# Two recurrent chains: summing head groups on VectorE after the transposes, instead of on TensorE before them

## The chip, the cores and the metric

The kernel runs on one core of one Trainium2 chip. Times are device microseconds (us) of one launch; the profile is one profiled execution of the same program. TensorE is called PE in the profile, its weight loads PEld, VectorE DVE, ScalarE ACT, GpSimd POOL; SPq is the queue of SyncE, from which most DMA transfers of this kernel are issued, in the order of the program.

## The reference, cut to what matters

The program computes a value and all its gradients. The part that decides here is a recurrence over 64 segments of 32 rows, with 8 memory rows handed from each segment to the next:

```python
for s in range(n_seg):                      # 64 segments, one after another
    h = concat([mem, x[s*32:(s+1)*32]])     # 8 + 32 rows of 512
    q, k, v = h@Wq, h@Wk, h@Wv              # 32 heads of 128
    p = softmax(mask(q@k.T * scale))
    o = einsum('bhte,hed->btd', p@v, Wo)    # a sum over 32 heads
    mem = o[:, :8]                          # the next segment waits for this
    outs.append(o[:, 8:])
```

The gradient runs the same chain backwards: the gradient of the eight memory rows is handed from segment s to segment s-1. There is also a dense squared-ReLU branch, which the change doesn't touch.

## The kernel before

The kernel has six stages: the dense branch, the projections of everything that doesn't depend on the memory ("left"), the forward chain (about 500 to 1375 us), a left backward stage, the backward chain (about 1605 to 2606 us), and the weight gradients. Each chain has 64 steps. Four steps make a block, which shares loads and "left" work (operations with the prefix `L.`). Steps are numbered 0 to 3 within a block, in order of execution.

The sum over 32 heads at the end of a step is made in two parts. TensorE adds up eight heads for each of four head groups, so that the result R lies in one PSUM bank with the groups on different partitions: 4 groups x 32 rows = 128 partitions, 512 columns. The four groups are then added, and the result turned so that the 512 columns lie on partitions, as the next projection wants them:

```python
def sum_ops(o, alloc, R4, F, st, pre=""):
    def sm():                                  # add the four groups: sel is a 0/1 matrix, 128 x 32
        ps["n"] = alloc("ps_sum")
        for c in range(DC):                    # 4 column blocks of 128
            nc.tensor.matmul(ps["n"][SEG*c:SEG*c+SEG, 0:P], lhsT=sel[:],
                             rhs=R4()[:, c*P:(c+1)*P], start=True, stop=True, ...)
    def sF():                                  # PSUM -> SBUF, 128x128
        ps["F"] = F()
        ENGS[pre + "sF"](ps["F"][:], ps["n"][:, 0:P])
    def sT():                                  # one float32 transpose
        nc.tensor.transpose(ps["n"][:, P:2*P], ps["F"][:], identF[:])
        st["sum"] = ps["n"][:, P:2*P].rearrange("p (c r) -> p c r", c=DC)
    ...
def ra():                                      # PSUM -> SBUF, all 512 columns, on ScalarE
    st["R4"] = fo.tile([P, D], F32, name="R4", tag="R4s")
    ENGS["ra"](st["R4"][:], ps["R"][:])
def HTf():                                     # the next memory rows: X (forward) or GT (backward)
    ENGS["HT"](block(b1)["X"][:, :, j1*SEG:j1*SEG+M], st["sum"][:, :, 0:M])
o["xt"] = lambda: ENGS["xt"](B_["XT"][:, :, j, M:SEG], st["sum"][:, :, M:SEG])   # the other 24 rows
```

The order in which operations are issued is written by hand, one string for each of the four steps. Each engine executes its own operations in that order. The strings end with the tail of the step: `ra sm sF sT HT`.

Of the kernel before, what the change touches and what calls it, by code (L numbers as in the profile page):

```python
# [8 lines left out]
ALU = mybir.AluOpType  # L9
AX = mybir.AxisListType  # L10
BF16 = mybir.dt.bfloat16
# [15 lines left out]
def kernel(  # L27
# [126 lines left out]

    sel = const.tile([P, SEG], F32, name="sel")
    nc.vector.tensor_reduce(sel[:], identF[:].rearrange("p (g r) -> p r g", g=HG), axis=AX.X, op=ALU.add)
# [325 lines left out]
    def sum_ops(o, alloc, R4, F, st, pre=""):  # L482

        ps = {}

        def sm():
            ps["n"] = alloc("ps_sum")
            for c in range(DC):
                nc.tensor.matmul(ps["n"][SEG * c:SEG * c + SEG, 0:P], lhsT=sel[:], rhs=R4()[:, c * P:(c + 1) * P],  # L489
                                 start=True, stop=True, tile_position=(0, SEG * c), skip_group_check=True)  # L490

        def sF():
            ps["F"] = F()
            ENGS[pre + "sF"](ps["F"][:], ps["n"][:, 0:P])

        def sT():
            nc.tensor.transpose(ps["n"][:, P:2 * P], ps["F"][:], identF[:])
            st["sum"] = ps["n"][:, P:2 * P].rearrange("p (c r) -> p c r", c=DC)
        o["sm"], o["sF"], o["sT"] = sm, sF, sT
# [92 lines left out]
    def play(order, n, steps, lefts, step, blk, last={}):  # L592
# [20 lines left out]
        "q0mm xt- L.lv L.ex0 q0ev L.mst- k0mm L.mx1 L.sb1 L.ex1 k1mm k1ev q1mm q0fl k0ev L.su0 k0fl L.su1 "  # L613
        "q1ev L.rc0 k1fl q0Te L.lq+ q1fl k0Te soP- k1Te s0 q1Te mx0 L.pm0 s1 km sb0 mx1 ex0 L.sm- soV- sb1 "
        "L.sF- soN ex1 v1mm ld- v0mm su0 rc0 su1 rc1 pm0 L.sT- ld tu0 pm1 tu1 kl+ v1ev L.lm v0ev L.ldL+ w0 "
        "L.xt- ob0 L.BT- oa0 L.rc1 soP L.tu0 w1 ob1 g0 oa1 g1 ra L.W0 sm L.out- L.oa0 sF L.ob0 sT HT",
        "k0mm L.hl++ L.pm1 q1mm q0mm ld k0ev xt- q1ev q0ev k1mm soV- k0fl q0fl L.tu1 k1ev k0Te q1fl q0Te k1fl k1Te s0 "
        "q1Te mx0 sb0 km s1 mx1 L.W1 ex0 sb1 su0 rc0 L.ob1 kl+ soN ex1 v0mm v0ev su1 L.oa1 v1mm pm0 rc1 tu0 w0 "
        "v1ev pm1 tu1 ob0 oa0 soV w1 ob1 g0 oa1 L.t3 g1 ra sm sF sT HT",
        "q0mm k0mm xt- q1mm k1mm q0ev q0fl q1ev k0ev soP- q0Te k0fl q1fl k1ev k1fl k0Te s0 q1Te k1Te mx0 L.u0- "  # L620
        "sb0 s1 v0mm mx1 sb1 ex0 ex1 su0 v0ev rc0 v1mm L.u3 su1 L.G0 rc1 pm0 pm1 L.t2 tu0 v1ev tu1 w0 ob0 L.t1 "
        "oa0 w1 g0 oa1 ob1 L.sx- L.ra0 L.u2 soP ld km g1 ra sm soN sF sT HT",
        "q0mm k0mm L.hs+ q0ev k1mm xt- q1mm q0fl k0ev kl q0Te k0fl k1ev k1fl L.u1 L.otr L.lo q1ev q1fl k0Te s0 k1Te "
        "q1Te mx0 s1 sb0 soV- ex0 L.t0 mx1 km sb1 su0 ex1 v1mm kl+ v0mm rc0 su1 rc1 pm0 tu0 L.mtr L.G1 v1ev "
        "v0ev pm1 tu1 L.lb w0 ob0 soN oa0 L.S0+ L.mx0+ w1 g0 oa1 ob1 g1 L.sb0+ ra L.ra1 sm sF L.S1+ sT HT")
    ENGS = on_engines(
        "L.oa0 L.oa1 L.ob0 L.ob1 L.sF L.xt k1Te k1ev oa1 ob0 q0ev q1ev ra v0ev v1ev",
        "HT L.pm0 L.pm1 L.ra0 k0Te k0ev oa0 ob1 pm0 pm1 q0Te q1Te sF xt")
    with sb("fw", 1) as fw, psum("fr", 4) as fr, psum("fpp", 1) as fpp, \
# [47 lines left out]
        def block(b):  # L677

            if b not in blk:
                shapes = {"kL": (fs, [P, KH, HG, NL], BF16), "OT": (fs, [P, HG, KH, SPB, SEG], BF16),  # L680
                          "X": (fs, [P, DC, P], BF16),
                          "kM": (fo, [P, KH, HG, NL], BF16), "vTM": (fo, [P, KH, HG, NL], BF16),
                          "XT": (fs, [P, DC, SPB, SEG], F32), "qL": (fo, [P, KH, HG, NL], BF16),
                          "VL": (fo, [P, GW], BF16), "vM": (fo, [P, GW], BF16), "EL": (fo, [P, KH, KW], BF16),
                          "OTL": (fo, [P, KH, HG, NL], BF16),
                          "bb": (fo, [P, D], BF16), "R4": (fo, [P, D], F32), "F": (fo, [P, P], F32)}

                def make(n):
                    pool, shape, dt = shapes[n]
                    return pool.tile(shape, dt, name=n, tag=n)  # L690
                blk[b] = Tiles(make)
            return blk[b]

        def left(b):
# [22 lines left out]
            for p in range(2):  # L717
# [21 lines left out]
                def G_(p=p):  # L739
# [5 lines left out]
            sum_ops(o, big, lambda: B_["R4"], lambda: B_["F"], st, "L.")  # L745
            o["xt"] = lambda: ENGS["L.xt"](B_["XT"][:, :, :, 0:M],
                                                st["sum"].rearrange("p c (j t) -> p c j t", j=SPB))
# [32 lines left out]
        def fwd(s):  # L780
# [80 lines left out]
            def ra():  # L861
                st["R4"] = fo.tile([P, D], F32, name="R4", tag="R4s")
                ENGS["ra"](st["R4"][:], ps["R"][:])
            o["ra"] = ra
            sum_ops(o, big, lambda: st["R4"], lambda: fo.tile([P, P], F32, name="F", tag="Fs"), st)

            def HTf():
                if s + 1 < NSEG:
                    b1, j1 = divmod(s + 1, SPB)
                    ENGS["HT"](block(b1)["X"][:, :, j1 * SEG:j1 * SEG + M], st["sum"][:, :, 0:M])  # L870
            o["HT"] = HTf
            o["xt"] = lambda: ENGS["xt"](B_["XT"][:, :, j, M:SEG], st["sum"][:, :, M:SEG])
# [40 lines left out]
    with sb("ls", 3) as ls, sb("lo", 1) as lo_, psum("lpp", 1) as lpp, psum("lr", 4) as lr:  # L913
# [87 lines left out]
        "o0mm o0ev xt- L.xt- o1mm o0fl vp0 L.lq o1ev o0te o1fl s0 vea0 veb0 o1te ldq- ldn- L.qo ldk- vtr vg0 "  # L1001
        "vlb0 d10 vla0 vp1 d20 d30 s1 L.G0 veb1 L.H0 d11 vlb1 vla1 d40 vea1 d21 tu0 kp0 kea0 klb0 keb0 d31 vg1 "
        "d41 kla0 qp0 qea0 qeb0 ldp kg0 tu1 kp1 kea1 klb1 L.sx- keb1 kla1 qg0 qp1 ldn qea1 qeb1 L.ra0 kg1 qg1 "
        "ra L.G1 sm vc sF L.H1 sT HT",
        "L.ra1 o0mm ldk- o1mm o0ev vtr o0fl o0te vp0 veb0 xt- o1ev vlb0 vla0 L.ktr vea0 s0 o1fl vp1 o1te L.G2 "
        "d10 d20 veb1 s1 vlb1 d30 vg0 d40 vea1 tu0 ldq- vla1 kp0 vg1 d11 kea0 kla0 d21 klb0 keb0 d31 d41 L.vtr "
        "qp0 qeb0 ldp qea0 tu1 vc kg0 kp1 kea1 qg0 keb1 kla1 klb1 qp1 kg1 qeb1 qea1 qg1 L.H2 ra sm sF sT L.ra2 "
        "HT",
        "xt- o0mm o0ev o1mm o0fl o1ev ldn- ldq- ldk- vp0 o1fl o0te s0 vlb0 veb0 d10 vla0 vea0 d20 d30 o1te vp1 "
        "vg0 vlb1 vtr s1 L.G3 vc vla1 veb1 d40 vea1 tu0 L.vst d11 d21 kp0 klb0 kea0 keb0 kla0 d31 vg1 L.kst d41 "  # L1010
        "qp0 qeb0 qea0 tu1 kg0 kp1 kea1 keb1 qg0 kla1 klb1 qp1 L.qtr kg1 qeb1 qea1 qg1 ra L.H3 sm sF sT ldp ldn "
        "HT",
        "L.ra3 o0mm L.qst o0ev L.ldt+ o1mm xt- o0fl L.gl+ o1ev vp0 o1fl o0te vlb0 vea0 vla0 s0 veb0 o1te vp1 "
        "d10 d20 d30 veb1 s1 d11 vg0 ldk- vlb1 d40 tu0 vea1 vtr L.gs+ vla1 ldq- d21 L.sm kp0 klb0 vc vg1 keb0 "
        "d31 L.sF kea0 kla0 d41 qp0 L.vo+ qeb0 tu1 kg0 qea0 L.ldv+ kp1 qg0 keb1 kla1 klb1 kea1 qp1 L.ldk+ qeb1 "
        "qea1 ldp kg1 L.ko+ qg1 ra sm sF L.sT sT HT")
    ENGS = on_engines(
        "L.ra0 L.sF kea0 kea1 kla0 kla1 o0ev o1ev o1te qea0 qeb1 ra sF vea0 vea1 veb1 vla0 vla1 vlb1 "
        "xt",
        "HT L.xt keb0 keb1 klb0 klb1 o0te qea1 qeb0 veb0 vlb0")  # L1020
    with sb("bq", 1) as bq, sb("bs", 2) as bs, sb("bt", 1) as bt, psum("bpp", 1) as bpp, psum("br", 4) as br:
# [11 lines left out]
        def block(b):  # L1033
            if b not in blk:
                shapes = {"gkL": (bs, [P, KH, HG, NL], BF16), "gvL": (bs, [P, KH, HG, NL], BF16),
                          "gqL": (bt, [P, KH, HG, NL], BF16), "PG": (bt, [P, 1, KH, KW], BF16), "GL": (bt, [P, 1, KH, KW], BF16),
                          "gOL": (bt, [P, GW], BF16), "qNL": (bt, [P, GW], BF16), "vTL": (bt, [P, KH, HG, NL], BF16),
                          "XT": (bs, [P, DC, SPB, SEG], F32), "R4": (bt, [P, D], F32), "F": (bt, [P, P], F32),
                          "gv": (bt, [P, HG, KH, SPB, SEG], BF16), "gk": (bt, [P, HG, KH, SPB, SEG], BF16),
                          "gq": (bt, [P, HG, KH, SPB, SEG], BF16)}  # L1040

                def make(n):
                    pool, shape, dt = shapes[n]
                    return pool.tile(shape, dt, name="b_" + n, tag=n)
                blk[b] = Tiles(make)
            return blk[b]

        def left(b):
# [15 lines left out]
            for i in range(4):  # L1064
# [12 lines left out]
                else:  # L1077
                    o["ra%d" % i] = lambda i=i: nc.vector.tensor_tensor(out=B_["R4"][:], in0=ps["R", i][:],
                                                                        in1=B_["R4"][:], op=ALU.add)
            sum_ops(o, big, lambda: B_["R4"], lambda: B_["F"], st, "L.")  # L1080
            o["xt"] = lambda: ENGS["L.xt"](B_["XT"][:, :, :, 0:M],
                                                st["sum"].rearrange("p c (j t) -> p c j t", j=SPB))
# [33 lines left out]
        def bwd(s):  # L1116
# [96 lines left out]
            def ra():  # L1213
                st["R4"] = bt.tile([P, D], F32, name="R4", tag="R4s")
                ENGS["ra"](st["R4"][:], ps["R"][:])
            o["ra"] = ra
            sum_ops(o, big, lambda: st["R4"], lambda: bt.tile([P, P], F32, name="F", tag="Fs"), st)

            def HTf():
                if s > 0:  # L1220
                    b1, j1 = divmod(s - 1, SPB)
                    ENGS["HT"](gts[b1][:, :, j1 * SEG:j1 * SEG + M], st["sum"][:, :, 0:M])
                else:
                    ps["S0"] = bq.tile([P, DC, M], F32, name="gm0")
                    nc.vector.tensor_copy(ps["S0"][:], st["sum"][:, :, 0:M])
            o["HT"] = HTf

            def xtf():
                ENGS["xt"](B_["XT"][:, :, j, M:SEG], st["sum"][:, :, M:SEG])
# [173 lines left out]
```

## Time and profile before

| what | value |
|---|---|
| time | 3289.62 us median of 4 runs (3287.35 to 3292.55) |
| profiled span | 3266.8 us |
| forward chain, mean step | 13.99 us |
| backward chain, mean step | 15.85 us (steps 0 to 3: 18.86, 14.11, 14.28, 16.39) |
| tail, from last gather matmul to the memory rows written | 2.14 to 2.18 us forward, 2.17 to 2.31 us backward |

The profiled run was 0.6% faster than the median of the timed ones, so spans and medians are not to be mixed. Step times are the distances from one writing of the memory rows (X or GT) to the next.

The page of the kernel before, its span, busy times, the chain of waits by engine, and one group of instructions (line, engine, operation, tiles, shapes, count, busy us, mean ns, idle before it):

```profile
span 3266.8 us, 115469 instructions
PE 2704.2 (83%) x51673; PEld 1338.9 (41%) x51768; DVE 1220.4 (37%) x3526; ACT 1017.1 (31%) x2492; POOL 193.7 (6%) x345
PE 57%; DMA 13%; SPq 13%; DVE 7%; issue 5%; ACT 5%; ACTq 0%; POOLq 0%; POOL 0%; DVEq 0%
L489 PE MATMUL ps_sum<-R,sel 128*32 128x128 f32 x1152 | 61.2, 285 | 58.4 <-ACT R L421 53.0
```

TensorE is the busy engine, but the chain that ended last also runs through DMA and its queue for a quarter of the span.

The timeline of the kernel before around the end of one forward step (start, length in us, engine, line, operation, out<-in; in brackets the idle time before it and what ended it):

```profile
907.13 0.59 ACT L421 COPY R<-ps_R 128x512 f32<-128x512 f32 x1 [1.49 <-PE ps_R L478]
907.76 0.43 PE L489 MATMUL ps_sum<-R,sel 128*32 128x128 f32 x8 [0.74 <-ACT R L421]
908.26 0.29 DVE L424 COPY F<-ps_sum 128x128 f32<-128x128 f32 x1 [2.52 <-PE ps_sum L489]
908.61 0.33 PE L497 MATMUL ps_sum<-identF,F 128*128 128x128 f32 x1 [0.41 <-DVE F L424]
908.97 0.19 DVE L424 CAST X<-ps_sum 128x32 bf16<-128x32 f32 x1 [0.42 <-PE ps_sum L497]
909.08 0.25 DVE L424 COPY XT<-ps_sum 128x96 f32<-128x96 f32 x1
909.22 2.13 PE L437 MATMUL ps_proj<-Wqkv,X 128*32 128x512 bf16 x36 [0.28 <-DVE X L424]
```

Five operations follow one another with nothing beside them, each released by the one before. From the end of the gather to X being written is 2.14 us.

The list of waits of TensorE in the backward chain of the kernel before (us in total, times, longest; "issue" is time in which no semaphore is shown to be waited for), two of its lines:

```profile
PE b_pp L563 <- issue: 45.8, 34, 4.7
...
PE b_pp L563 <- DMA b_qN<-S_A: 12.3, 11, 2.7
```

The last line is a load (qN, 256 KB) from memory, which TensorE needs in the middle of a step.

### The profile page before, as it was taken

Reading aid. Unit: us, or ns where it says so; the run is one execution under the profiler, and the core shown is the slowest. Engines: PE = TensorE matmul, PEld = TensorE weight load, DVE = VectorE, ACT = ScalarE, POOL = GpSimd, SP = SyncE. Lnnn points to the kernel's source line nnn. Section 1 sums busy time; section 2 is a strip of 40 time slices with the busy share of each in tenths; the row PEclk is TensorE's granted clock in tenths of the full one; section 3 lists DMA queues with packets and bytes.
Section 4 is the critical chain, followed back from the end, with each engine's and each line's share of the span. In section 5 each row is a group of like instructions: output and inputs, shape, how many; then the busy total and the mean of one; then the engine's idle time right before and its main releaser. Section 6 shows DMA issues by size and latency. Waiting matters only on the chain.

```text
span 3266.8 us, 115469 instructions
## 1 busy us (share of the span) xinstructions
PE 2704.2 (83%) x51673; PEld 1338.9 (41%) x51768; DVE 1220.4 (37%) x3526; ACT 1017.1 (31%) x2492; POOL 193.7 (6%) x345
## 2 busy tenths in 40 slices
PE   8898778888888888834688888888888866999998
PEld 4453334444444444412344344344344423444444
DVE  4440035555655555523344344444444400010001
ACT  3331124444444444412333333333333401111111
POOL 0000000000000000000000010010000000000000
PEclk9999899999999999966799999999999988999999
DMA  9958894676667676689668666666776699999993
GB/s 254 283 145 312 293 291 114 165 179 162 185 164 184 161 184 161 171 235 256 185 164 210 166 164 181 189 164 172 190 183 172 173 260 199 205 186 224 187 187 91
DMA packets 890915, 633.20 MB, mean 194 GB/s; under 512 B 659745, under 2 KB 748466, under 8 KB 881074
## 3 DMA queue, kind: packets, MB, share of 16 engines
q1 hardware_dynamic: 890418, 625.81, 77.0%
q8 instruction: 406, 6.65, 0.8%
q14 instruction: 91, 0.75, 0.1%
HBM read 227.16 MB, written 250.10 MB: 146 GB/s over the span
## 4 chain that ended last, share of the span: by engine, by line
PE 57%; DMA 13%; SPq 13%; DVE 7%; issue 5%; ACT 5%; ACTq 0%; POOLq 0%; POOL 0%; DVEq 0%
PE ps_gR L478 11%; PE ps_proj L437 11%; PE ps_gw L1364 8%; SPq L1289 6%; PE b_pp L563 3%; PE ps_R L478 3%; DMA S_GOL<-l_gON 3%; PE ps_tr L167 2%; ACT R L421 2%; PE ps_sum L489 2%; PE ps_L L406 2%; DMA out_dram<-wt 2%; PE ps_w L366 2%; PE ps_w L386 1%; PE ps_RL L1071 1%
## 5 line engine op out<-in xcount | busy, mean ns | idle before, releaser
L1364 PE MATMUL ps_gw<-gn,HNc 128*128 128x512 bf16 x1881 | 416.5, 380 | 8.3 <-ACT wt L1339 6.3
L437 PE MATMUL ps_proj<-Wqkv,X 128*32 128x512 bf16 x6144 | 361.9, 385 | 18.2 <-DVE X L424 17.9
L1364 PEld LDWEIGHTS <-HNc 128*128 128x128 bf16 x1920 | 188.2, 98 | 231.9 <-issue 9.5
L421 ACT CAST f_N<-ps_proj 128x512 bf16<-128x512 f32 x320 | 185.4, 583 | 258.0 <-PE ps_proj L437 243.7
L1339 ACT CAST wt<-ps_gw 128x512 bf16<-128x512 f32 x126 | 69.5, 591 | 541.8 <-DMA out_dram<-wt 353.1
L437 PEld LDWEIGHTS <-X 128*32 128x32 bf16 x6144 | 156.9, 98 | 174.7 <-DVE X L424 29.9
L1322 DVE TENSOR_TENSOR gx<-ps_rows,gb 128x512 f32<-128x512 f32 x16 | 11.1, 692 | 427.5 <-PE ps_rows L1320 396.8
L1364 PE MATMUL ps_gw<-GOc,gn 128*128 128x512 bf16 x627 | 142.2, 387 | 19.2 <-DMA gn<-S_ON 18.3
L478 PE MATMUL ps_gR<-WT,b_gq 128*32 128x512 bf16 x2048 | 145.2, 401 | 7.8 <-issue 7.5
L478 PE MATMUL ps_gR<-WT,b_gk 128*32 128x512 bf16 x2048 | 145.8, 404 | 5.8 <-issue 5.7
L478 PE MATMUL ps_gR<-WT,b_gv 128*32 128x512 bf16 x2048 | 142.5, 393 | 7.6 <-issue 7.5
L437 PE MATMUL ps_proj<-WoT,GT 128*32 128x512 bf16 x2048 | 125.6, 388 | 22.5 <-DVE GT L424 17.9
L478 PE MATMUL ps_R<-Wo,OT 128*32 128x512 bf16 x2048 | 127.1, 390 | 0.0
L1145 POOL COPY b_vT<-b_vl 128x1024 bf16<-128x1024 bf16 x64 | 66.7, 1042 | 905.9 <-PE ps_sc L458 521.4
L421 ACT CAST gON<-ps_proj 128x512 bf16<-128x512 f32 x128 | 75.0, 586 | 118.9 <-PE ps_proj L437 115.2
L489 PE MATMUL ps_sum<-R,sel 128*32 128x128 f32 x1152 | 61.2, 285 | 58.4 <-ACT R L421 53.0
L1364 PEld LDWEIGHTS <-gn 128*128 128x128 bf16 x640 | 63.6, 100 | 96.4 <-DMA gn<-S_ON 18.6
L406 PE MATMUL ps_L<-Wqkv,XL 128*128 128x512 bf16 x376 | 84.8, 385 | 18.2 <-DMA XL<-S_XL 16.8
L421 ACT CAST b_gq<-b_pp 128x256 bf16<-128x256 f32 x128 | 47.7, 373 | 161.4 <-PE b_pp L563 153.3
L421 ACT CAST b_gk<-b_pp 128x256 bf16<-128x256 f32 x128 | 47.8, 373 | 150.7 <-PE b_pp L563 115.5
L424 DVE CAST b_gq<-b_pp 128x256 bf16<-128x256 f32 x128 | 54.4, 425 | 107.0 <-PE b_pp L563 102.8
L437 PEld LDWEIGHTS <-GT 128*32 128x32 bf16 x2048 | 49.5, 98 | 78.4 <-DVE GT L424 30.0
(214 smaller groups left out, 4427.9 us busy)
## 6 DMA issues: line engine op xcount, KB each, us to landing
S_A<-f_N SPq DMA_DIRECT2D x64, 512.0 KB
out_dram<-wt SPq DMA_DIRECT2D x154, 128.0 KB
S_A<-f_N SPq DMA_DIRECT2D x64, 256.0 KB
S_ON<-OC SPq DMA_DIRECT2D x64, 256.0 KB
b_qN<-S_A SPq DMA_DIRECT2D x64, 256.0 KB
b_kN<-S_A SPq DMA_DIRECT2D x64, 256.0 KB
S_GB<-b_gv SPq DMA_DIRECT2D x16, 1024.0 KB
S_GB<-b_gk SPq DMA_DIRECT2D x16, 1024.0 KB
```

The lines of the kernel that those rows point to most:

```text
L167: nc.tensor.transpose(ps_ap, in_ap, ident[base:base + k, base:base + k])
L366: nc.tensor.matmul(ps[:], lhsT=aN[:, rc, fc * P:(fc + 1) * P], rhs=gN[:, rc, :], start=(rc == 0), stop=(rc == TC - 1))
L406: nc.tensor.matmul(ps[:], lhsT=XL[:, dc, q * P:(q + 1) * P], rhs=Wqkv[:, dc, c0:c0 + 512], start=(dc == 0), stop=(dc == DC - 1))
L421: nc.scalar.copy(out, in_)
L437: nc.tensor.matmul(ps[32 * g:32 * g + 32, :], lhsT=hT[:, dc, :], rhs=W[:, dc, c:c + 4 * P], start=(dc == 0), stop=(dc == DC - 1), tile_pos ...
L478: nc.tensor.matmul(R[32 * g:32 * g + 32, :], lhsT=XT(k, g), rhs=W[:, g * KH + k, :], start=(first and k == 4 * h), stop=(last and k == 4 * ...
L489: nc.tensor.matmul(ps["n"][SEG * c:SEG * c + SEG, 0:P], lhsT=sel[:], rhs=R4()[:, c * P:(c + 1) * P], start=True, stop=True, tile_position= ...
L563: nc.tensor.matmul(o, lhsT=N_[32 * g:32 * g + m, kk * P:(kk + 1) * P], rhs=X(kk)[32 * g:32 * g + m], start=(i == 0), stop=(i == len(jobs) ...
L1145: nc.gpsimd.tensor_copy(vT[:, :, :, 0:SEG], C["vl"][:])
L1289: nc.sync.dma_start_transpose(t_[:, b, :].rearrange("p (k e) -> p k e", k=KH), blocks(b)[:, g].rearrange("p k r -> p (k r)"))
L1339: nc.any.tensor_copy(wt[:], ps[:])
L1364: nc.tensor.matmul(ps[:], lhsT=l(rc), rhs=r(rc), start=(n == 0), stop=(n == RC_ALL - 1))
```

## The change

The intent: the four groups lie on partitions, so before the transpose only TensorE can add them. After the transpose they lie along the free dimension, and VectorE can add them while it writes the memory rows, which it has to do anyway. So R is copied in two halves on two engines, each half is turned by two float32 transposes, and one strided reduction per output replaces the copy. The selecting matmuls, the copy F and the matrix `sel` go. The same is done for the left blocks.

```diff
-    def sum_ops(o, alloc, R4, F, st, pre=""):   # sm, sF, sT as above
+    def turn_ops(o, alloc, R4, st):
+        def tT(c):
+            if c == 0:
+                st["T"] = alloc("ps_sum")
+            nc.tensor.transpose(st["T"][:, c * P:(c + 1) * P], R4()[:, c * P:(c + 1) * P], identF[:])
+        for h in range(2):
+            o["t%s" % "ab"[h]] = lambda h=h: [tT(c) for c in (2 * h, 2 * h + 1)]
+    def left_sums(XT, T):
+        for c in range(DC):
+            nc.vector.tensor_reduce(XT[:, c, :, 0:M], T[:, c*P:(c+1)*P].rearrange("p (g j t) -> p j t g", ...),
+                                    axis=AX.X, op=ALU.add)
+    def over_groups(out, T, rows):
+        nc.vector.tensor_reduce(out, T[:].rearrange("p (c g r) -> p c r g", c=DC, g=HG)[:, :, rows],
+                                axis=AX.X, op=ALU.add)
...
-            def ra():
-                ENGS["ra"](st["R4"][:], ps["R"][:])
+            def ra(h):                            # ra: columns 0-255 on ScalarE, rb: 256-511 on VectorE
+                c = slice(h * 2 * P, (h + 1) * 2 * P)
+                ENGS["r%s" % "ab"[h]](st["R4"][:, c], ps["R"][:, c])
...
-                    ENGS["HT"](block(b1)["X"][:, :, j1 * SEG:j1 * SEG + M], st["sum"][:, :, 0:M])
+                    over_groups(block(b1)["X"][:, :, j1 * SEG:j1 * SEG + M], st["T"], slice(0, M))
-            o["xt"] = lambda: ENGS["xt"](B_["XT"][:, :, j, M:SEG], st["sum"][:, :, M:SEG])
+            o["xt"] = lambda: over_groups(B_["XT"][:, :, j, M:SEG], st["T"], slice(M, SEG))
...
 (order strings: the tail "ra sm sF sT HT" becomes "ra rb ta tb HT"; the left "L.sm L.sF L.sT" become
  "L.ta L.tb"; nothing else changes place. xt backward and L.xt forward move from ScalarE to VectorE.
  Cut here: the allocation of R4 in ra, a low precision flag in over_groups.)
```

The transposes `ta tb` stand where `sT` stood. Pieces of other work that stood between `sm` and `sT` now come before the first transpose.

## The prediction

> **What bounds the kernel now.** The busy table gives PE 83% and DVE 37% of 3266.8 us. The forward memory chain (about 488 to 1386 us) takes 13.99 us a step and the backward chain (1605 to 2623 us) 15.85 us, 64 steps each. Every step ends with the same tail (timeline, last gather matmul to the next memory rows): ScalarE copy R 0.59, eight selecting matmuls 0.47, copy F 0.29, transpose 0.33, VectorE cast X/GT 0.19, with 0.02 to 0.08 between them: 2.14 to 2.29 us. The chain of waits holds the R copy for 2.1% of the span, about 116 of 128 tails.
>
> **What the change does.** It drops the selection, F and one transpose, and adds four float32 transposes (four take 0.66 us in ps_rows), a strided VectorE reduction, and a halved R copy. The halves read one PSUM bank. "PSUM — Partial Sum Buffer", "PSUM bank collisions raise a hardware error", says two engines may not touch one bank and quadrant together; the built program makes VectorE's half wait for ScalarE's. No run here shows a collision. So the halves run in series: 0.37 (128x256 ScalarE casts) + 0.43 (VectorE) + 0.06, not 0.59.
>
> Reductions took 0.32 us for 160 elements, so 128 should take about 0.28; the one reduction with the same stride (sel, SBUF) took 0.37. I take 0.33 for the memory rows, 0.55 to 0.8 for the other 384 elements (copy before: 0.25), and 1.0 to 1.4 for the four of a left block (one 0.27 copy before).
>
> New tail: 0.08 + 0.37 + 0.06 + 0.43 + 0.05 + 0.46 (two transposes) + 0.02 + 0.33 = 1.80 us, about 0.35 saved in an undisturbed step.
>
> **What gives it back.**
> - Forward step 0 of a block: the left reductions stand on VectorE before the OT copy that g0 needs: about +1.1 us, less some 0.5 of slack where PE waits for vM. Residual addition (0.69) now runs after R's second half, so that tail gains only 0.2.
> - Forward step 3 and backward step 1: the 0.69 us left addition runs between that half and the memory reduction: gain 0.15.
> - Backward step 0: both pieces of left gather (1.3 us) now precede the transposes: gain 0.
> - Backward step 1: the row reduction moves from idle ScalarE to VectorE behind a copy; four PSUM buffers rotate, so the first score matmuls may wait for it: up to +1 us.
>
> Per block, forward -0.35 -0.35 -0.15 +0.8, backward +0.1 +0.85 -0.35 -0.35: about +0.2 us, times 16: +3 us.
>
> **Predicted time:** 3292 us, range 3250 to 3335; faster by over 2% 0.06, within 2% 0.86, slower by over 2% 0.08.
>
> **What would show each step.** Timeline: VectorE's R half starts after ScalarE's ends; memory tail near 1.8 us in forward steps 1 and 2, near 2.0 in forward 3; reduction 128x32<-128x128 of 0.28 to 0.37 us; forward step 0 longer by 0.5 to 1 us, its OT copy behind the left reductions; backward step 1's first ps_sc matmul after the row reduction. Busy table: DVE about 1355 us, ACT about 945.
>
> **What would make it wrong.** Slack in the two bad steps: 30 us faster. Reductions far over 1 ns an element, or VectorE delays reaching the softmax string: slower. Waits for qN loads (15 of them, 31 us together in the list of waits) may swallow backward gains.

## The result, and the profile after

| | before | after |
|---|---|---|
| time, median of 4 runs each | 3289.62 us | 3257.55 us (3253.77 to 3261.32) |
| ratio | | 0.9902, 95% interval 0.9885 to 0.9919 |
| profiled span | 3266.8 us | 3252.0 us |
| forward step, mean | 13.99 us | 13.69 us |
| backward step, mean | 15.85 us | 15.79 us |
| tail, forward | 2.14 us | 1.76 us |
| tail, backward, steps 1 to 3 | 2.17 us | 1.70 us |

Ratios here and below are the mean time of one kernel's fast runs over that of the other's of the same rounds, so not quite the ratio of the medians quoted. The changed kernel was run again later on another chip, beside a run of the kernel before there: 3243.93 against 3271.44 us, ratio 0.9919 [0.9883, 0.9954]. The worth of the change is thus 0.8 to 1%: 27 to 32 us. The medians of the kernel before differed by up to 0.6% between jobs, so kernels are compared only with the kernel before of their own job.

From the first to the last memory rows, the forward chain shrank from 867.6 to 849.0 us, the backward chain from 983.0 to 978.8 us. The last stage, which the change does not touch, lay between 654 and 670 us in the profiled runs; that is why two spans alone would not settle a difference of 20 us.

The page after:

```profile
span 3252.0 us, 113992 instructions
PE 2723.4 (84%) x50873; PEld 1356.1 (42%) x50968; DVE 1332.7 (41%) x3765; ACT 952.7 (29%) x2316; POOL 193.7 (6%) x345
L484 PE MATMUL ps_sum<-identF,R 128*128 128x128 f32 x576 | 116.2, 297 | 24.6 <-ACT R L418 21.7
```

The predicted 1355 us for DVE and 945 us for ACT came out as 1332.7 and 952.7. The transposes cost TensorE 116.2 us, more than the selections (61.2) and the old transposes (47.6) together, and the time still fell: PE's busy time in the tail is not what is scarce.

The timeline after, at the end of a forward step:

```profile
968.59 0.37 ACT L418 COPY R<-ps_R 128x256 f32<-128x256 f32 x1 [1.49 <-PE ps_R L475]
969.00 0.42 DVE L421 COPY R<-ps_R 128x256 f32<-128x256 f32 x1 [1.20 <-ACT R L418]
969.02 0.90 PE L484 MATMUL ps_sum<-identF,R 128*128 128x128 f32 x4 [0.53 <-ACT R L418]
969.95 0.29 DVE L497 TENSOR_REDUCE X<-ps_sum 128x32 bf16<-128x128 f32 x1 [0.53 <-PE ps_sum L484]
970.16 0.55 DVE L497 TENSOR_REDUCE XT<-ps_sum 128x96 f32<-128x384 f32 x1
970.30 1.91 PE L434 MATMUL ps_proj<-Wqkv,X 128*32 128x512 bf16 x32 [0.38 <-DVE X L497]
```

The two halves of R run one after the other: VectorE starts at 969.00, when ScalarE's 0.37 us are over, and its wait is put down to "ACT R". The reduction of 128 elements to 32 takes 0.29 us. The tail is 1.76 us, 0.38 less than before.

If every one of 128 tails had passed on about 0.4 us, some 50 us would have been gained. Measured: the forward chain passed on 0.30 us a step, the backward chain 0.07. The experiments ask where the backward gain went.

The list of waits of TensorE in the backward chain after:

```profile
PE b_pp L562 <- issue: 39.4, 37, 4.0
PE b_pp L562 <- DMA b_qN<-S_A: 26.1, 14, 3.3
...
PE ps_gR L475 <- issue: 23.5, 18, 5.3
...
PE b_pp L562 <- DVE b_gvL L421: 4.5, 16, 0.4
```

The waits for qN grew from 12.3 to 26.1 us, all in step 3 of the blocks (0.82 to 1.74 us a block). This is not by itself the loss: in the same steps the holds under "issue" fell from 1.42 to 0.51 us a block, so that the two together were 2.24 us before and 2.25 us after.

### The profile page after: what moved, and what is told of

Its sections match the earlier page's. It is cut to its first block, busy times and chain, and to the rows that moved or that the text cites. A ratio compares the mean times of both kernels' runs of the same rounds, so it can differ in the third digit from the quotient of the medians.

```text
span 3252.0 us, 113992 instructions
## 1 busy us (share of the span) xinstructions
PE 2723.4 (84%) x50873; PEld 1356.1 (42%) x50968; DVE 1332.7 (41%) x3765; ACT 952.7 (29%) x2316; POOL 193.7 (6%) x345
## 5 line engine op out<-in xcount | busy, mean ns | idle before, releaser
L484 PE MATMUL ps_sum<-identF,R 128*128 128x128 f32 x576 | 116.2, 297 | 24.6 <-ACT R L418 21.7
L484 PEld LDWEIGHTS ps_sum<-identF,R 128*128 128x128 f32 x576 | 58.4, 141 | 97.0 <-ACT R L418 53.7
```

The lines of the kernel that those rows point to most:

```text
L484: nc.tensor.transpose(st["T"][:, c * P:(c + 1) * P], R4()[:, c * P:(c + 1) * P], identF[:])
```

## The experiments

The texts name theories by letters; the two that decide are these. Theory A: the shorter tail is passed on in the forward chain, but in the backward chain the step that follows is bounded by something which started before the tail, above all the qN load, so a shorter tail only lengthens the wait for it. Theory D: the backward chain is paced by its DMA traffic, directly and through delayed instruction fetches; and with less traffic the change would gain more there. Rivals for single steps are told where they stand. Four kernels ran in each of three jobs, each job on one chip: the first four below, the next four, and the last four.

### The change in one chain only

Both kernels keep the old and the new operations, and each chain takes one set:

```diff
# e1: forward from after, backward from before.   e2: forward from before, backward from after.
-            turn_ops(o, big, lambda: st["R4"], st)          # in one chain only
+            sum_ops(o, big, lambda: st["R4"], ..., st)
-  ... qg1 ra rb ta tb HT
+  ... qg1 ra sm sF sT HT
```

> Only the forward chain is changed, the backward chain is the old one. Theory A (read from the two traces: forward steps fell from 13.99 to 13.69 us, backward steps only from 15.85 to 15.79, because in backward the shorter tail is given back as longer waits of PE inside the step): this kernel keeps most of the gain, 0.993 of the time before (about 3267 us), forward step 13.7, backward step 15.85. Rival B (both chains gain alike and the flat backward mean is chance of one trace): 0.995 or more, with a gain no larger than that of the backward half alone.

> Only the backward chain is changed. Theory A: 0.998 of the time before (3283 us, within 6 us of it), although the tail of backward steps 1 to 3 is again 1.70 instead of 2.17 us; the list of waits shows PE waiting longer for qN than before (26 us against 12). Rival B: 0.995 or less, backward step 15.5 us or less.

Measured: forward alone 3251.48 us, ratio 0.9947 [0.9916, 0.9979]; backward alone 3266.03 us, ratio 0.9987 [0.9955, 1.0019] (before there: 3268.97 us). The steps agree: 13.64 us a forward step in the first (13.97 in the second), 15.79 a backward step in the second (15.81 in the first). The intervals of the two ratios overlap, so the times alone don't place the gain; the traces do. From the first to the last memory rows, the forward chain took 865.9 to 871.2 us in the four kernels with the old forward chain, and at most 853.3 us in the ten with a new one. The gain is in the forward chain, and tails that are shorter by 0.47 us (0.1 in step 0) give next to nothing in the backward chain. Theory A's first half stands.

### The copy of R: halves on one engine, or no halves

```diff
# e3: both halves on ScalarE, in both chains
-        "... oa1 ob0 q0ev q1ev ra v0ev v1ev",      "... q0Te q1Te rb")
+        "... oa1 ob0 q0ev q1ev ra rb v0ev v1ev",   "... q0Te q1Te")
# e4: no halves: ra copies 512 columns on ScalarE, rb does nothing
+            def whole():
+                ENGS["ra"](st["R4"][:], ps["R"][:])
+            o["ra"], o["rb"] = whole, lambda: None
```

> The changed kernel with both halves of the R copy on ScalarE instead of one on ScalarE and one on VectorE. Theory A (the halves are serial anyway because they read one PSUM bank, and a second ScalarE copy follows its first by about 0.28 us while the hand-over to VectorE costs 0.06 + 0.43): tail about 1.5 us instead of 1.76 in forward steps and 1.70 in backward steps; time 0.984 of before (3237 us), most of it in the forward chain. Rival C (the halves overlap enough that the VectorE half is free): tail no shorter, time at or above the changed kernel's 0.990.

> The changed kernel with one whole R copy on ScalarE (0.59 us), no halves; all four transposes follow it. Theory A (halving over two engines saves nothing, 0.37 + 0.06 + 0.43 in series, of which the first two transposes hide some 0.2): tail 0.08 + 0.59 + 0.05 + 0.66 + 0.02 + 0.29 = 1.69 us, time within 0.3% of the changed kernel. Rival C (halving is what shortens the tail): tail 1.9 us or more, time 0.994 or more of before.

The timelines of a forward step's end, first with both halves on ScalarE, then with the whole copy:

```profile
962.61 0.65 ACT L418 COPY R<-ps_R 128x256 f32<-128x256 f32 x2 [1.49 <-PE ps_R L475]
963.04 0.71 PE L484 MATMUL ps_sum<-identF,R 128*128 128x128 f32 x4 [0.53 <-ACT R L418]
963.79 0.29 DVE L497 TENSOR_REDUCE X<-ps_sum 128x32 bf16<-128x128 f32 x1 [1.97 <-PE ps_sum L484]
```

```profile
966.59 0.58 ACT L418 COPY R<-ps_R 128x512 f32<-128x512 f32 x1 [1.49 <-PE ps_R L475]
967.23 0.65 PE L484 MATMUL ps_sum<-identF,R 128*128 128x128 f32 x4 [0.75 <-ACT R L418]
967.92 0.29 DVE L497 TENSOR_REDUCE X<-ps_sum 128x32 bf16<-128x128 f32 x1 [2.12 <-PE ps_sum L484]
```

Two halves on one engine overlap: 0.65 us for both, less than 0.37 + 0.42 on two engines. The tail is 1.57 us with halves on ScalarE, 1.73 with the whole copy, against 1.76 (1.70 backward) in the change as given. So giving the second half to VectorE saves nothing in the tail over not halving at all; what saves is the rest of the change. The times: 3236.87 us, ratio 0.9901 [0.9872, 0.993], and 3243.2 us, ratio 0.9919 [0.9885, 0.9953]. The first is a miss for my expectation: the tail became nearly as short as expected (1.57 for about 1.5 us), but the ratio stayed within the interval of the change as given. Its forward step is 13.54 us, 0.1 to 0.15 below the changed kernel's, and its backward step 15.82, not shorter at all. Why 0.2 us less of tail gives only 0.1 to 0.15 in the forward chain was not settled.

### Earlier loads of qN

In step 3 of a backward block, the qN load is issued late, behind stores and transposed loads. SyncE's queue in the kernel before and after, around the start of such a step (GT of the step before was written at 2098.49 in the first, and at 2071.97 in the second; line, operation, out<-in):

```profile
2094.41 0.33 SPq L1135 DMA_DIRECT2D b_kN<-S_A  x1
...
2099.01 1.27 SPq L1140 DMA_TRANSPOSE b_vl<-S_A  x1
2100.32 0.61 SPq L1059 DMA_DIRECT2D S_GM<-GT  x1
2100.97 0.62 SPq L1134 DMA_DIRECT2D b_qN<-S_A  x1
```

```profile
2068.49 0.33 SPq L1132 DMA_DIRECT2D b_kN<-S_A  x1
...
2072.40 2.12 SPq L1137 DMA_TRANSPOSE b_vl<-S_A  x1
2074.57 0.60 SPq L1057 DMA_DIRECT2D S_GM<-GT  x1
2075.22 0.62 SPq L1131 DMA_DIRECT2D b_qN<-S_A  x1
```

In both, kN is issued before the tail, and qN about 6.6 us after kN; the queue never waits for GT to be finished before it goes on, apart from the store S_GM, which comes late enough not to care. Measured from the last gather matmul of the step before, over 15 blocks, kN is issued 1.8 us before it in both kernels, qN 4.5 us after it in the kernel before and 4.6 in the changed one, and the first matmul that needs qN starts at 8.45 and 8.48 us. The tail in between is 0.47 us shorter, and the matmul starts at the same time. This is the parallel path. The experiment moves only the load, in the changed kernel (e5) and in the kernel before (e6):

```diff
-        "L.ra3 o0mm L.qst o0ev ... vla1 ldq- d21 ..."       # backward, step 3
+        "ldq- L.ra3 o0mm L.qst o0ev ... vla1 d21 ..."
```

> The changed kernel with one edit: in backward step 3 of a block the load of qN is issued first of that step's loads instead of after the turned v rows and two others (its buffer is free by then). Theory A (the shorter tail is given back in step 3 as a longer wait for this load, 1.7 to 1.95 us a block in all four kernels with the changed backward tail, 0.65 to 0.82 in the two with the old tail): the wait falls under 0.3 us, step 3 from 16.3 to about 14.8 us, backward mean from 15.79 to about 15.4, time about 0.984 of before. Rival D (DMA traffic as a whole paces the backward blocks; the wait only moves to another load or to a hold of PE that no semaphore explains): the qN wait falls but backward mean stays at 15.7 or more, time 0.990.

> The same edit in the kernel before. Theory A: backward mean falls by the 0.8 us of the old qN wait over four steps, to about 15.65 us, time 0.996; then the change is worth about 0.25 us a backward step once the load is out of the way, against 0.07 now. Rival D: backward mean stays at 15.8, time 1.000.

Measured: 3245.78 us, ratio 0.9889 [0.9856, 0.9922], and 3273.14 us, ratio 0.9978 [0.9951, 1.0005] (before there: 3283.13 us). With the early load the first matmul on qN starts at 6.74 us after the last gather with the new tail, and at 7.42 us with the old one: now the tail's difference of 0.47 us does arrive, with something on top, and step 3 is shorter with the new tail (15.76 against 16.42 us). The waits of TensorE in the backward chain of e5 begin with these lines, and one for qN is not among the first six:

```profile
PE b_pp L562 <- issue: 46.6, 41, 5.0
PE ps_gR L475 <- issue: 29.5, 25, 3.0
```

So the wait for qN is gone, as theory A says, but not the time: "issue" grew from 39.4 and 23.5 us in the changed kernel to 46.6 and 29.5. In step 3 these holds went from 0.51 to 2.02 us a block. The mean backward step was 15.59 us, between the 15.4 of theory A and the 15.7 or more of theory D. Both have a part: removing one late load uncovers the next limit. The total with the early load is not distinguishable from the change as given.

In e6, with the old tail, the mean backward step was 15.75 us and not the 15.65 of theory A. With the load early in both, the change is thus worth 0.16 us a backward step in one pair of traces, where theory A said 0.25 and the kernels as given differ by 0.07. The times don't confirm even that: e5 and e6 lie 27 us apart, no more than the kernels as given. So the early load lets step 3 keep its shorter tail, but that the whole program gains more from the change in this way is not shown.

### Two suspected costs of the changed order

In backward step 1 the row reduction (`xt`, 0.55 us) now stands on VectorE between two copies, where ScalarE had done a 0.24 us copy before. VectorE's lines in such a step, before and after:

```profile
2006.60 0.42 DVE L424 CAST b_gv<-b_pp 128x256 bf16<-128x256 f32 x1
2006.94 0.21 DVE L424 CAST b_gvL<-b_pp 128x64 bf16<-128x64 f32 x1
```

```profile
2109.41 0.42 DVE L421 CAST b_gv<-b_pp 128x256 bf16<-128x256 f32 x1
2109.75 0.55 DVE L497 TENSOR_REDUCE b_XT<-ps_sum 128x96 f32<-128x384 f32 x1
2110.21 0.21 DVE L421 CAST b_gvL<-b_pp 128x64 bf16<-128x64 f32 x1
```

The copy b_gvL comes 0.80 us after b_gv instead of 0.34, and TensorE waits for it: 4.5 us in 16 waits in the list above, 0.28 us a block. The experiment e7 moves the reduction to the start of the step:

```diff
-        "L.ra1 o0mm ldk- o1mm o0ev vtr o0fl o0te vp0 veb0 xt- o1ev vlb0 ..."     # backward, step 1
+        "L.ra1 o0mm xt- ldk- o1mm o0ev vtr o0fl o0te vp0 veb0 o1ev vlb0 ..."
```

In forward step 0, the four reductions of the left block stand on VectorE ahead of the copy OT, which the gather needs. VectorE's lines, before and after:

```profile
890.50 0.45 DVE L471 STREAM_TRANSPOSE ET<-E 128x256 bf16<-128x256 bf16 x1
890.87 0.39 DVE L424 CAST OT<-f_pp 128x256 bf16<-128x256 f32 x1
...
891.81 0.43 DVE L424 CAST OT<-f_pp 128x256 bf16<-128x256 f32 x1
```

```profile
938.25 0.45 DVE L468 STREAM_TRANSPOSE ET<-E 128x256 bf16<-128x256 bf16 x1
938.62 0.85 DVE L491 TENSOR_REDUCE XT<-ps_sum 128x32 f32<-128x128 f32 x4
939.39 0.41 DVE L421 CAST OT<-f_pp 128x256 bf16<-128x256 f32 x1
...
940.36 0.43 DVE L421 CAST OT<-f_pp 128x256 bf16<-128x256 f32 x1
```

The first OT copy starts 1.14 us after the transpose of E starts, instead of 0.37. Four reductions take 0.85 us, about 0.2 us for each that follows another. The experiment e8 puts them behind both OT copies, and moves the left row transposes (L.BT) and the residual addition (L.out) behind the gather and the tail:

```diff
-   "... w0 L.xt- ob0 L.BT- oa0 L.rc1 soP L.tu0 w1 ob1 g0 oa1 g1 ra rb L.W0 L.out- L.oa0 L.ob0 ta tb HT"
+   "... w0 ob0 oa0 L.rc1 soP L.tu0 w1 ob1 L.xt- g0 oa1 g1 ra rb L.BT- L.W0 L.oa0 L.ob0 ta tb HT L.out-"
```

> The changed kernel with the 384 element row reduction of backward step 1 moved from between the two copies of the first v product to the start of the step, where VectorE idles. Theory A (that place costs PE 0.28 us a block waiting for the copy behind it, and delays the score gradients by 0.35): step 1 from 13.99 to about 13.65 us, backward mean from 15.79 to 15.7, time 0.989. Rival: the delay is hidden by other PE work, or comes back in the step 3 wait: backward mean unchanged, time 0.990.

> The changed kernel with the four left reductions of forward step 0 moved behind the last OT copy of VectorE, their row transposes behind the gather and the residual addition behind the memory rows. Theory A (they hold up the OT copy, and with it the second outer product, by 0.6 us a block): forward step 0 from 14.39 (median) to about 13.9 us, forward mean from 13.69 to 13.57, time about 0.988 of before. Rival: the wait for vM and the loads sets step 0 anyway: 14.3, time 0.990.

Measured: 3253.44 us, ratio 0.9919 [0.9888, 0.9949], and 3253.96 us, ratio 0.991 [0.9881, 0.9938]. Neither is distinguishable from the change as given. In e7, step 1 of the backward blocks fell from 13.99 to 13.78 us, but the mean step stayed at 15.79 us. The wait for qN in step 3 was 2.11 us a block (1.74 before the edit), yet step 3 itself stayed at 16.24 us; step 0 was 0.22 us longer, about what two traces of one kernel differ by (the control: 0.14 in step 0, 0.39 in step 3). Where the gain went is not settled. In e8, the median of forward step 0 fell from 14.39 us (14.21 in the second trace of the changed kernel) to 14.05, while the tail of that step grew to 2.21 us: by the order, the left block's four transposes (L.BT) then stand on TensorE ahead of the tail's own. Its mean step 0, 14.68 us, is that of the control. So the cost in backward step 1 shows, and is small; the one in forward step 0 shows in the median alone.

### Less DMA traffic

Here the stores of the three gradient arrays of a block in the backward chain (1 MB each) are cut to a quarter, in the changed kernel (e9) and in the kernel before (e10). These two give wrong weight gradients (three of the outputs), with the same reads in the last stage from the part that is written.

```diff
-                o[n + "o"] = lambda ...: dma(S_GB[b, t], B_["g" + n][:].rearrange(...))
+                o[n + "o"] = lambda ...: dma(S_GB[b, t][:, 0:1], B_["g" + n][:, 0:1].rearrange(...))
-                                                blocks(b)[:, g].rearrange("p k r -> p (k r)"))
+                                                blocks(b)[:, 0].rearrange("p k r -> p (k r)"))
```

> The changed kernel, storing only one of the four head groups of the backward products (a quarter of 3 MB a block; the last stage reads that quarter four times, so three weight gradients are wrong on purpose). This takes 1.5 MB of 4.1 from backward step 3 and 0.75 of 3.5 from step 0. Theory D (DMA traffic in steps 3 and 0 holds up qN and the holds of PE that no semaphore explains, and these take back what the tail saves): step 3 from 16.3 to about 14.5 us, step 0 to about 18, backward mean about 15.1. Rival (the pace of steps 3 and 0 is set by something else): backward mean stays at 15.7 to 15.8.

> The same cut of the stores in the kernel before (wrong on purpose in the same way). Theory D: with the traffic gone the shorter tail of the change is kept, so this backward mean stays at least 0.25 us above that of the changed kernel with thin stores (about 15.35 to 15.4 against 15.1), where the full kernels differ by 0.07. Rival (the change loses its backward gain on the engines, through VectorE's added load): the two differ by less than 0.12.

Measured: 3203.92 us, ratio 0.979 [0.9754, 0.9826], and 3207.99 us, ratio 0.9803 [0.9769, 0.9838] (before there: 3271.44 us). The mean backward step fell to 14.87 us with the new tail and to 14.90 with the old. So the traffic does pace this chain, by about 0.9 us a step, in steps 0 and 3 (after: 19.14 to 16.44 and 16.25 to 15.45 us); the first half of theory D holds. But the difference between the two tails stayed 0.03 us a step: its second half falls, and the number is the one that the rival named (under 0.12). The rival's mechanism, added load on the engines, isn't shown by this: with thin stores, the new tail made steps 1 and 2 shorter by 0.15 and 0.52 us and step 3 longer by 0.51 (15.45 against 14.94). With thin stores the qN load is still issued at the same place: TensorE still waits 1.6 us a block for it with the new tail and 0.87 with the old, and the matmul on qN starts 8.39 and 8.37 us after the last gather. The wait in step 3 is set by where the load stands in the queue, and its size is not the DMA traffic's.

One thing here is unexplained. The times of e9 and e10 lie only 4 us apart, while those of the control and the kernel before in the same job lie 27 us apart. In the traces, the forward chain is shorter by 25 us with the new tail, as elsewhere, but the profiled run of e9 (3186.15 us) was 18 us faster than the median of its runs.

### All that helped, together

e11 takes e3, e5, e7 and e8 together, with L.BT placed behind the transposes so that it doesn't lengthen the tail; e12 is the changed kernel, unedited, as a control in the same job.

```diff
-   "... ld- ... w0 L.xt- ob0 L.BT- oa0 L.rc1 soP L.tu0 w1 ob1 g0 oa1 g1 ra rb L.W0 L.out- L.oa0 L.ob0 ta tb HT"
+   "... ld- ... w0 ob0 oa0 L.rc1 soP L.tu0 w1 ob1 L.xt- g0 oa1 g1 ra rb L.W0 L.oa0 L.ob0 ta tb L.BT- HT L.out-"
    (rb on ScalarE as in e3; ldq- first in backward step 3 as in e5; xt- early in backward step 1 as in e7)
```

> A version meant to beat both: the changed kernel with both R halves on ScalarE, the early qN load, the early row reduction of backward step 1, and in forward step 0 the left reductions behind the last OT copy, their row transposes while VectorE reduces the memory rows, the residual addition after that. Expected from the single edits: forward mean about 13.3 us (tail 1.58, step 0 about 13.8), backward about 15.5; time about 0.980 of before.

> The changed kernel itself, unaltered, on the same chip as the three others, as their control. Both theories: 0.990 of before, forward mean 13.7, backward 15.75 to 15.8; it tells how far traces and times of one kernel differ between chips.

Measured: 3212.84 us, ratio 0.9816 [0.9772, 0.9861], against the control's 3243.93 us, ratio 0.9919 [0.9883, 0.9954]. The runs of the two do not overlap (3191.40 to 3223.17 and 3234.12 to 3251.50). Its outputs are correct, and it beats both kernels; whether it is over 2% faster than the kernel before its interval leaves open. The mean forward step is 13.41 us (control 13.64), the backward one 15.53 (control 15.67). Each of the four edits alone gave at most 0.3%, within its interval; which of them the sum rests on, and how much they help each other, was not taken apart further.

## Why the prediction was right or wrong

The time lay in the predicted range and in the predicted class. That it did is in part luck, by the width of the range: it reached from 40 us faster to 45 us slower. The sum was 27 to 32 us faster where I had said 3 us slower. My list of what would make it wrong had this case, "Slack in the two bad steps: 30 us faster", and the terms show how far it was that.

**The tail: right.** "New tail: 1.80 us, about 0.35 saved in an undisturbed step": measured 1.76 us and 0.38 forward, 1.70 and 0.47 backward. The halves ran in series as said. Trainium skill, "PSUM — Partial Sum Buffer", section "PSUM bank collisions raise a hardware error", says why a schedule must keep two engines off one bank and quadrant. This trace shows the order, VectorE's half 0.04 us behind ScalarE's, and no collision. The halves on ScalarE alone (1.57 us) then showed that the tail doesn't need the split onto two engines. The reduction of 128 elements took 0.29 us (predicted 0.33), that of 384 0.55 (predicted 0.55 to 0.8).

**Forward step 0: the mis-sized term.** The prediction said "+0.8" for this step; its own terms, 1.1 less 0.5 of slack less 0.2 of tail, make 0.4. Measured: the median rose by 0.05 us (14.34 to 14.39) and the mean by 0.18; over all traces the mean was 14.92 us in the four kernels with the old forward chain and 14.87 in seven with the new one. Two sizes were off. The four left reductions took 0.85 us and not 1.0 to 1.4, because back to back they start about 0.2 us apart, which the single reduction I had measured did not show. And I had let the tail of that step gain only 0.2, as the residual addition of 0.69 us would stand behind R's second half; it ran while TensorE did the transposes, and the tail fell by the whole 0.38. In such a tail after the change, `bb` is the addition:

```profile
942.69 0.81 PE L484 MATMUL ps_sum<-identF,R 128*128 128x128 f32 x4
942.92 0.68 DVE L764 TENSOR_TENSOR bb<-ps_rows,bb 128x512 bf16<-128x512 f32 x1
943.53 0.29 DVE L497 TENSOR_REDUCE X<-ps_sum 128x32 bf16<-128x128 f32 x1
```

The delay of the OT copy itself was real: the distance between the two products that feed OT on TensorE (from the end of w0 to the start of w1) grew from 0.59 to 0.98 us in the mean of 15 blocks. It stayed at 0.56 us in 6 of the 7 blocks in which w0 itself was held up by 0.9 us or more, mostly waiting for a load (f_vLs): there the reductions ran beside that wait.

**Forward steps 1, 2 and 3.** Predicted -0.35, -0.35, -0.15; measured by medians -0.38, -0.39, -0.15. Steps 1 and 2 are right. Step 3 is right in the number only: I had the left addition lengthen its tail to about 2.0 us, but it too ran beside the transposes, and the tail fell from 2.18 to 1.76. The time up to the gather grew instead, from 11.45 to 11.72 us; why is not shown. The four steps together were predicted as -0.05 us a block. Measured by the mean step it was four times 0.30, 1.2 us a block, or 19 us in 16 blocks. This is most of the error in the sum; the backward chain has the rest, about 8 us.

**Backward step 1: predicted +0.85, measured -0.12 (control: -0.23).** The prediction said "the first score matmuls may wait for it: up to +1 us". They did not: the first score matmul starts 2.83 us after the memory rows, 2.81 before, although the reduction ends only at about 3.6. The rotation of PSUM buffers did not hold them up there. What did happen was smaller and elsewhere: the reduction delays the copy b_gvL, for which TensorE waits 0.28 us a block. The shorter tail of 0.47 us outweighs that.

**Backward step 3: predicted -0.35, measured 0 within the noise.** The means are 16.39 before and 16.25 after, but 15.84 in e1 with the old tail against 16.80 in e2 and 15.86 in the control with the new. The last sentence of the prediction, "Waits for qN loads may swallow backward gains", is what happened here, though I had put none of it into the sum. The wait for qN grew by 0.9 us a block between the two profiled kernels, but it took the place of holds under "issue". Counted together, the two were 1.98 us a block in the mean of the two traces with the old backward tail and the late load (before, e1), and 2.37 in the seven with the new one (after, e2, e3, e4, e7, e8, e12; 1.98 to 2.78): about 0.4 us more, nearly what the tail had saved.

The rest is in part the clock of TensorE. Trainium skill, "TensorE: Matmul & The Clock Gate", section "Why this matters for your kernels", asks for no idle gaps above about 3 us between bursts of matmuls. In this trace gaps of 2.0 to 2.5 us already were followed by 3.41 us at half clock in 6 of 10 cases in the changed kernel's backward chain (1 of 5 in the kernel before), counted where the half clock begins no later than 0.5 us after the gap; up to 1.9 us after it, they were 10 of 10 and 3 of 5. Gaps of 0.5 to 1.0 us never were so followed (0 of 18 and 0 of 38, apart from one inside a half-clock stretch already running). Of the 20 half-clock stretches of that chain, 19 begin during an idle time of over 1.9 us or at most 1.9 us after it. The waits for qN are often of that size: step 3 has 10 half-clock records in the changed kernel (control: 7) and 3 in the kernel before (4 in e1). The view by stretches of time, for one step 3 before and one after (PE, PEld, DVE, ACT, POOL busy us, then the granted clock, the DMA share and GB/s):

```profile
2098.49:2114.52 16.03, 12.42 (x378) 6.04 (x378) 7.31 (x23) 6.01 (x19) 1.48 (x2) 1.00 0.88 261
```

```profile
2071.97:2087.99 16.02, 13.44 (x368) 6.42 (x368) 7.68 (x24) 5.17 (x16) 1.39 (x2) 0.89 0.90 244
```

Two steps of equal length: in the one with the shorter tail TensorE was busy for 1.0 us more at a mean clock of 0.89, though its work is about the same (four transposes, 0.66 us, in place of a selection and a transpose, 0.43 + 0.33 us, once for the chain and once for the left block). Over the 15 blocks the mean clock of step 3 was 0.97 to 0.99 in kernels with the old tail there (before, e1, e10) and 0.91 to 0.95 with the new one (after, e2, e3, e4, e9); with the early load it was 0.97 with the new tail and 0.96 with the old (e5, e6). Read so, a longer idle time costs twice: once by itself and once by the slower matmuls after it. That the idle time causes the half clock is read from the order in the traces; no experiment set the length of the idle time alone.

**Backward step 0: predicted +0.1, measured +0.28 (control: +0.42).** Its tail gained 0.1 us, since two pieces of left gather stand before the transposes. In the middle of the step, the holds of TensorE under "issue" were longer: 2.58 us a block before, 3.09 after (control: 3.13).

**What "issue" is.** In the changed kernel's backward chain TensorE has 28 holds of over 0.7 us with no semaphore behind them, 59.4 us together (34 holds and 67.3 us in the kernel before). All 28 end 1.23 to 1.57 us after the end of a 16384-byte packet of the instruction queue, q8; if the two had nothing to do with each other, about 8% would fall into a window of 0.4 us, as such packets come every 5.2 us. With thin stores the holds fell to 20.4 us (15 holds). So it is likely that TensorE waits here for its next instructions, and that these wait behind data; no run moved the fetches alone. Trainium skill, "Runtime: NRT & Kernel Launch", section "Instruction fetch mechanics", says that instructions are fetched in blocks of 16 KiB and that the cost is "mostly hidden". The block size agrees with the packets in this trace. Most of the cost is hidden here too, for 28 holds stand against about 196 packets in that chain; the rest is not small. The sum of the holds is much the same in both kernels, so it does not explain the change's effect; they sit elsewhere, though: more in step 0 and fewer in step 3 after the change. They fit with e5 winning less than the wait that it removed.

**The sum.** Backward, predicted +0.25 us a block; measured -0.25 by the four step means of the two profiled kernels, and -5 us in the 64 steps when the traces of all kernels with one tail are averaged (15.83 before and e1; 15.76 after, e2, e8 and e12). Forward, averaged in the same way (14.01 and 13.68 us), about -21 us. Together about -26 us, of the 27 to 32 measured. By steps, in the same traces, backward steps 0 to 3 changed by +0.1, -0.2, -0.3 and +0.15 us, for tails shorter by 0.1, 0.47, 0.47 and 0.47. So half of what was lost, 0.6 of 1.2 us a block, was lost in step 3, where the qN load stands; the other half is spread over steps 0 to 2, and only the 0.2 us of e7 in step 1 was traced to a cause.

What stays open: where the backward chain loses the other half; why jobs on different chips differ by 0.6% for one kernel; why the still shorter forward tail of e3 passed on only half to three quarters of what it saved; and how early q loads would do together with fewer or better spread stores, which was not run.

## What to carry to other kernels

Shortening the serial tail of a step pays in full only if nothing that was started before the tail ends later: before counting on a gain, look up when each load that the next step needs is issued, and whether that moment moves with the tail. A queue that works in order (loads on one DMA queue, copies on one engine) can turn a saved wait into a longer wait somewhere else, and a longer idle time of TensorE can cost clock on top. Two engines reading one PSUM bank by halves ran in series in this program; one engine doing both halves, with the consumer starting after the first, was faster here (0.65 against 0.79 us of copying).

## What the Trainium skill lacked or had wrong

- "PSUM — Partial Sum Buffer": it says that two engines must not touch one bank and quadrant at once, but not what a split costs: halves of a 128x512 copy took 0.37 + 0.42 us in series on two engines, 0.65 us for both on ScalarE, and 0.58 us as one copy.
- "PSUM — Partial Sum Buffer", section "Specifications (TRN2)": it warns that a non-contiguous access pattern slows matmuls in PSUM, and gives no figure for what VectorE pays. Here the reduction over groups read PSUM at a stride of 32 float32 values, and 128 elements took 0.29 us, as long as a contiguous 128x128 copy (0.29 us); 384 took 0.55 us.
- "VectorE: DVE Perf Modes", section "Rules for kernel authors": it calls `tensor_reduce` the slowest operation of VectorE and says to expect "1×" of it. Read from PSUM in float32 this was no loss: 128 elements took no longer than the copy of as many, as above, so there the row is no reason to avoid it.
- "TensorE: Matmul & The Clock Gate", section "Why this matters for your kernels": the limit of about 3 us of idle time is too generous here; gaps of 2.0 to 2.5 us were followed within 0.5 us by 3.41 us or more at half clock in 6 of 10 cases (1 of 5 in the kernel before).
- "Runtime: NRT & Kernel Launch", section "Instruction fetch mechanics": it gives no figure for the fetches that are not hidden under DMA load; 28 holds of TensorE, 59.4 us together, ended 1.23 to 1.57 us after one of about 196 fetched packets of 16384 bytes.
- No page read gives the time of float32 transposes on TensorE: one 128x128 took 0.33 us from start to end, four in a row 0.65 us.
